# A gated mix of a recurrent attention and a feed-forward block: 32 output rows in one transfer instead of four

## The chip, the cores and the metric

The kernel runs on one core of a Trainium2 chip. Its measure is the time of one execution on the device, in microseconds (us). Five engines run side by side, each from its own instruction queue: TensorE (PE, with its weight loads as PEld), VectorE (DVE), ScalarE (ACT), GpSimd (POOL) and SyncE (SP). Data moves between device memory (HBM) and the on-chip memory of 128 partitions by DMA, on 16 DMA engines that all queues share. In this kernel SP issues the large weight loads, POOL nearly all small transfers.

## The reference

Two branches read the same 2048 rows of 1024 numbers and are mixed row by row with a gate.

```python
g = sigmoid((x * gate_w).sum(-1, keepdims=True))
return g * a + (1 - g) * b
```

Branch b is a feed-forward block, `gelu(x @ w_gate) * (x @ w_up) @ w_down`, with 3584 hidden units. Branch a is an attention that goes through the rows in 64 segments of 32, one after another, each with 8 rows of memory ahead of it:

```python
for s in range(n_seg):
    h = concatenate([mem, x[:, s*32:(s+1)*32, :]], axis=1)      # 8 + 32 rows
    q, k, v = h @ Wq, h @ Wk, h @ Wv                            # 32 heads of 128
    p = softmax(where(mask, q @ k.T * scale, -1e9))
    o = (p @ v) @ Wo
    mem = o[:, :8, :]
    outs.append(o[:, 8:, :])
```

The memory of a segment is the output of the one before, so the segments form a chain. All numbers are bfloat16 in HBM.

## The kernel before, in words

The first 600 us compute branch b for all rows and leave (1 - g) * b in a scratch tensor in HBM, `b_scr`, which is laid out by segment, column quarter and row. Then come the 64 segments, some 29 us each.

A segment keeps the 32 rows that are stationary for a matrix product in `hT`. The product has only 32 output rows, so four products run in four groups of 32 rows of a bank, one for each quarter of the columns. Hence the output of a segment stands in PSUM and in the tile `bo` as 128 partitions x 256 columns: partition 32 * q + r holds row r, columns 256 * q to 256 * q + 255.

The six projection weights and Wo do not fit on the chip. What stays lies in `arena`, `extra` and a few reused tiles; the rest streams through `ring`, ten slots of 1024 columns, in transfers of 512 or 256 KB that SP issues (`stream_next`, line 601) as soon as TensorE has freed a slot (`slot_free`, line 622). Each segment needs 18.5 units of 512 KB.

Of the 40 rows of a segment, 8 memory rows and 32 of its own, the block in `hT` holds rows 8 to 31 and then the memory rows; the output of the memory rows is the memory of the next segment. The first 8 rows of a segment do not hang on the recurrence as a projection does, and so their projections are made apart, for four segments at a time, by the jobs "q", "k" and "v" (the "ext" rows); the "o" job, in every fourth segment, makes the output of 32 ext rows, which goes through the tile `pn` (seen as `pnz`) that the softmax also writes (line 1045). The output of a segment leaves as the 32 rows `of[s * 32 + 8 : s * 32 + 40]`: the last 8 of them lie where the next segment's first rows belong, and the ext transfers (1343) write those rows afterwards, once the earlier transfers have landed.

The order of the work is written out by hand in the loop over s (line 798). Every operation is recorded by `op` with the keys that it reads and writes, and `_Sched` turns them into semaphore waits: an operation waits for the earlier writer of what it reads and for the earlier readers of what it writes. A DMA gets a semaphore of its own name (`dsem`), and whoever depends on it waits for the landing.

At the end of segment s the order is: ACT copies the accumulated output to `rows` (line 1306), TensorE transposes the memory rows (1317), DVE copies them into `hT` (1322), which lets TensorE go on with segment s + 1. Then DVE adds the gated output to `bo`, which holds (1 - g) * b (line 1325). POOL, which waits for that, issues the output transfers (1332), one for each column quarter: 32 partitions x 256 columns to 32 rows of `out`, 512 bytes each. With an "o" job DVE also writes `pn` (1336), and POOL issues four transfers of 32 ext rows (1343), whose side in HBM is 4 segments x 8 rows x 256 columns.

Behind these in POOL's queue stand, for segment s + 1: two loads of ext values into `vt` (723), one of ext queries and keys into `qkst` (711), a store of a job's result (852 or 877), and the load of the next `bo` (`load_b`, 737), which has to wait until the output transfers of segment s have read `bo`. Later in the segment come two more loads of `vt`, one of `qkst`, and that of the next rows into `hT` (412). The last segment issues its output from SP and ACT instead.

Of the kernel before, what the change touches and what calls it, by code (L numbers as in the profile page):

```python
# [26 lines left out]
class _Sched:  # L27
# [10 lines left out]
    def op(self, eng, mk, r=(), w=(), dsem=None):  # L38
        o = _Op(eng, mk, dsem)
        deps = []  # L40
        if eng == "pool" and dsem is None:
            w = [*w, ("pool",)]
        for k in r:
            deps += self.w.get(k, ())
            if k[0] == "P":
                deps += [x for x in self.r.get(k, ()) if x.eng != eng]
        for k in w:
            deps += self.w.get(k, ())
            deps += self.r.get(k, ())
        for k in r:  # L50
            self.r.setdefault(k, []).append(o)
        for k in w:
            self.w[k] = [o]
            self.r[k] = []
        seen = set()
        for d in deps:
            if d is o or id(d) in seen:
                continue
            seen.add(id(d))
            if d.eng == eng and d.dsem is None and (eng == "pe" or eng == "sp"):  # L60
                continue
            o.deps.append(d)
            d.sig = True
        self.ops.append(o)
        return o
# [63 lines left out]
def bass_gated_mix__memory_aug_recurrent_mem_tr__geglu_ffn__prompt_kernel(  # L129
# [16 lines left out]
    of = out.flatten_outer_dims()  # L146
# [4 lines left out]
    SEG = 32  # L151
# [12 lines left out]
    EXT = 8  # L164
# [3 lines left out]
    with ExitStack() as es:  # L168
# [14 lines left out]
        def SB(shape, dt, name):  # L183
            return es.enter_context(nc.sbuf_tensor(name, list(shape), dt))
# [17 lines left out]
        bo = SB([128, 256], BF16, "bo")  # L202
# [16 lines left out]
        def P(i):  # L219
            return ("P", i)  # L220

        g = _Sched()
        op = g.op
# [15 lines left out]
        def A(c):  # L239
# [6 lines left out]
           r=[("ident",)], w=[("ident",)])  # L246
# [57 lines left out]
        for b0 in (0, 64):  # L304
            op("pool", lambda e, b0=b0: e.affine_select(
                out=mask[b0:b0 + SEG, 0:NR], in_=mask[b0:b0 + SEG, 0:NR], compare_op=ALU.is_ge, fill=NEG,
# [3 lines left out]
                out=mask[b0 + SEG:b0 + L, SEG:L], in_=mask[b0 + SEG:b0 + L, SEG:L], compare_op=ALU.is_ge, fill=NEG,  # L310
# [3 lines left out]
        for side in range(2):  # L314
            op("pool", lambda e, side=side: e.memset(bm[64 * side:64 * side + L, side:side + 1], 1.0),
               r=[("bm",)], w=[("bm",)])
# [411 lines left out]
        def rows_of(s):  # L728
            n = SEG if s + 1 < NSEG else NR
            v = of[s * SEG + EXT:s * SEG + EXT + n, :]  # L730
            return [(v[:, q * 256:(q + 1) * 256], bo[32 * q:32 * q + n, :]) for q in range(4)]
# [12 lines left out]
        def first_rows(t, j, q):  # L744
            return t.rearrange("(g s r) d -> g s r d", s=GR, r=SEG)[j, :, 0:EXT, q * 256:(q + 1) * 256]
# [52 lines left out]
        for s in range(NSEG):  # L798
# [333 lines left out]
            if s == 0:  # L1132
                emit_P("q", 0, ALL[:5])
                op("pe", lambda e: e.matmul(PB[B_S][:, 0:320], lhsT=pnz[:, 0:128], rhs=pnz, start=True, stop=True),
                   r=[("init", "pn")], w=[P(B_S)])
# [10 lines left out]
                   w=[("bo", x) for x in range(4)])  # L1146
# [158 lines left out]
            if s + 1 < NSEG:  # L1305
                op("act", lambda e, B_O=B_O: e.activation(rows[:, 0:256], PB[B_O][:, 0:256], ACTF.Copy),
                   r=[P(B_O)], w=[("rows",)])
# [5 lines left out]
            if s + 1 < NSEG:  # L1313
# [12 lines left out]
                out=bo[:, :], in0=PB[B_O][:, 0:256], scalar=gseg[:, s:s + 1], in1=bo[:, :], op0=ALU.mult, op1=ALU.add),  # L1326
               r=[P(B_O)] + [("gseg", "%s%d" % (k, q)) for k in "ab" for q in range(4)], w=[("bo", x) for x in range(4)])
            for put, bank in ends:
                put(bank)
            last = s == NSEG - 1  # L1330
            for x, (d, b) in enumerate(rows_of(s)):
                op(("sp", "act")[x % 2] if last else "pool", lambda e, d=d, b=b: e.dma_start(d, b),  # L1332
                   r=[("bo", x)], w=[("out", s, x)], dsem="%s%d" % ("end" if last else "out", x))
            if "o" in jobs:
                j = jobs["o"]
                op("dve", lambda e, j=j: e.scalar_tensor_tensor(
                    out=pnz[:, 0:256], in0=PB[B_X][:, 0:256], scalar=ge[:, j:j + 1], in1=rowsx[:, 0:256],
                    op0=ALU.mult, op1=ALU.add),
                   r=[P(B_X)] + [("gseg", "e%d%d" % (q, u)) for q in range(4) for u in range(GR)] + RX,
                   w=[("pn", 0), ("pn", 2 * SEG)])  # L1340
                for q in range(4):
                    op(("sp", "act")[q % 2] if last else "pool",
                       lambda e, q=q, j=j: e.dma_start(first_rows(of, j, q), pnz[32 * q:32 * q + 32, 0:256]),
                       r=[("pn", 0)] + [("out", x, q) for x in range(max(0, j * GR - 1), j * GR + GR - 1)],
                       w=[("oute", j, q)], dsem="%s%d" % ("ende" if last else "oute", q))
# [43 lines left out]
```

## Time and profile before

| what | value |
|---|---|
| median of 3 runs | 2498.48 us (2494.85 to 2501.15) |
| profiled execution | 2490.87 us, of which the span is 2489.0 us |
| granted TensorE clock, mean | 0.988 |
| stretch 700 to 2440 us | PE busy 1539.88 us, POOL 533.10 us, DMA share 1.00, 367 GB/s |
| output transfers (line 1332) on POOL | 252 issues, 125.8 us |
| ext output transfers (line 1343) on POOL | 60 issues, 35.5 us |

A row of a group in the profile reads: line, engine, operation, tile written, tile read, count; then busy time and mean time of one; then the idle time of the engine just before these instructions and what ended it. A row of the list of waits reads: who waited for whom, us in total, times, longest. In the DMA row each digit is the mean busy share of the 16 DMA engines in one of 40 equal slices, 9 for 90% or more. The rows of queues give packets, MB, and the time of their packets as a share of 16 engines' span. A timeline row gives start and duration in us; one that ends in x4 stands for four instructions in a row. "To landing" is the time from the issue of a DMA to the last of the 16 increments of its semaphore.

### The profile page before, as it was taken

Reading aid. Unit: us, or ns where it says so; the run is one execution under the profiler, and the core shown is the slowest. Engines: PE = TensorE matmul, PEld = TensorE weight load, DVE = VectorE, ACT = ScalarE, POOL = GpSimd, SP = SyncE. Lnnn points to the kernel's source line nnn. Section 1 sums busy time; section 2 is a strip of 40 time slices with the busy share of each in tenths; the row PEclk is TensorE's granted clock in tenths of the full one; section 3 lists DMA queues with packets and bytes.
Section 4 is the critical chain, followed back from the end, with each engine's and each line's share of the span. In section 5 each row is a group of like instructions: output and inputs, shape, how many; then the busy total and the mean of one; then the engine's idle time right before and its main releaser. Section 6 shows DMA issues by size and latency. Waiting matters only on the chain.

```text
span 2489.0 us, 77539 instructions
## 1 busy us (share of the span) xinstructions
PE 2256.3 (91%) x33977; PEld 1112.8 (45%) x33977; DVE 1169.8 (47%) x3435; ACT 930.9 (37%) x2196; POOL 653.4 (26%) x1162
## 2 busy tenths in 40 slices
PE   9999999999889888988988898888889888889887
PEld 4444444444444444444444444444444444444443
DVE  5626264451444444544454544444444444455444
ACT  4314132221334343434443444434444434444433
POOL 1010103102232323233323323332323232323222
PEclk9999999999899999999999999999999999999988
DMA  8727354468999999999999999999999999999997
GB/s 273 257 71 256 97 179 123 144 229 302 322 348 365 365 371 348 373 359 379 375 377 354 374 366 374 352 356 367 375 370 378 365 363 376 362 377 374 371 362 281
DMA packets 328689, 797.10 MB, mean 320 GB/s; under 512 B 52728, under 2 KB 116456, under 8 KB 327584
## 3 DMA queue, kind: packets, MB, share of 16 engines
q1 hardware_dynamic: 284336, 736.78, 81.2%
q0 software_dynamic: 43872, 55.31, 7.1%
q8 instruction: 267, 4.37, 0.7%
q14 instruction: 70, 0.57, 0.1%
q10 hardware_dynamic: 144, 0.06, 0.0%
HBM read 764.52 MB, written 37.22 MB: 322 GB/s over the span
## 4 chain that ended last, share of the span: by engine, by line
PE 58%; DMA 26%; DVE 9%; ACT 4%; issue 3%; POOL 0%; SPq 0%; DVEq 0%; POOLq 0%
DMA ring<-w_scr 25%; PE pba L948 7%; PE pbb L948 7%; PE pbc L835 5%; PE pbb L1107 3%; PE pbe L1055 3%; PE pba L1107 2%; PE pbe L992 2%; PE pba L449 2%; PE pbb L449 2%; PE pbh L449 2%; PE pbg L449 2%; PE pbf L449 2%; PE pbe L449 2%; PE pbd L449 2%
## 5 line engine op out<-in xcount | busy, mean ns | idle before, releaser
L948 PE MATMUL pba<-arena,hT 128*32 128x512 bf16 x4416 | 350.6, 384 | 0.0
L948 PE MATMUL pbb<-arena,hT 128*32 128x512 bf16 x4416 | 342.6, 385 | 0.3 <-issue 0.3
L999 DVE COPY qk<-pbe 128x512 bf16<-128x512 bf16 x129 | 89.2, 692 | 363.3 <-PE pbe L992 358.6
L723 POOL DMA_DIRECT2D vt<-v_scr x252 | 147.9, 591 | 371.6 <-PE pbf L1066 234.1
L1038 ACT ACTIVATE pbd<-pbd 104x160 f32<-104x160 f32 x256 | 71.9, 281 | 432.2 <-DVE pbd L1036 432.2
L1060 DVE COPY ptb<-pbe 80x320 bf16<-80x320 bf16 x256 | 82.1, 321 | 240.5 <-PE pbe L1055 240.5
L1332 POOL DMA_DIRECT2D out_dram<-bo x252 | 125.8, 506 | 246.1 <-DVE bo L1325 244.9
L948 PE MATMUL pba<-ring,hT 128*32 128x512 bf16 x1542 | 153.2, 388 | 28.9 <-DMA ring<-w_scr 27.7
L835 PE MATMUL pbc<-arena,xe 128*32 128x512 bf16 x2208 | 174.4, 380 | 0.7 <-ACT rowsx L849 0.5
L948 PE MATMUL pbb<-ring,hT 128*32 128x512 bf16 x1536 | 151.9, 390 | 25.3 <-DMA ring<-w_scr 23.5
L954 ACT ACTIVATE rows<-pba 128x512 bf16<-128x512 f32 x128 | 76.6, 598 | 234.2 <-PE pba L948 234.2
L948 PEld LDWEIGHTS pba<-arena,hT 128*32 128x32 bf16 x4416 | 111.8, 97 | 97.9 <-issue 5.6
L1045 DVE TENSOR_TENSOR pn<-pbd,rr 104x256 bf16<-104x256 f32 (+1 forms) x512 | 142.3, 319 | 27.7 <-DMA out_dram<-pn 19.4
L948 PEld LDWEIGHTS pbb<-arena,hT 128*32 128x32 bf16 x4416 | 109.7, 97 | 93.0 <-issue 8.0
L954 ACT ACTIVATE rows<-pbb 128x512 bf16<-128x512 f32 x128 | 76.6, 598 | 173.7 <-PE pbb L948 173.6
L877 POOL DMA_DIRECT2D qk_scr<-rowsx x60 | 47.5, 791 | 344.2 <-DVE rowsx L874 281.6
L1107 PE MATMUL pba<-arena,oT 128*32 128x256 bf16 x2176 | 120.9, 281 | 14.1 <-ACT oT L1074 12.5
L1107 PE MATMUL pbb<-arena,oT 128*32 128x256 bf16 x2176 | 121.9, 279 | 12.7 <-ACT oT L1074 10.8
L1055 PE MATMUL pbe<-ident,pn 104*80 104x104 bf16 x1024 | 95.4, 216 | 40.9 <-DVE pn L1045 21.6
L1107 PE MATMUL pba<-ring,oT 128*32 128x256 bf16 x1792 | 107.0, 277 | 20.0 <-DMA ring<-w_scr 19.1
L1039 DVE TENSOR_REDUCE rs<-pbd 104x4 f32<-104x160 f32 x256 | 83.0, 324 | 88.9 <-ACT pbd L1038 88.9
L1107 PE MATMUL pbb<-ring,oT 128*32 128x256 bf16 x1792 | 113.5, 275 | 7.9 <-DMA ring<-w_scr 7.2
(260 smaller groups left out, 4355.2 us busy)
## 6 DMA issues: line engine op xcount, KB each, us to landing
ring<-w_scr SPq DMA_DIRECT2D x973, 512.0 KB, 6.3
ring<-w_scr SPq DMA_DIRECT2D x486, 256.0 KB, 5.9
arena<-in_B_w_gate_dram SPq DMA_DIRECT2D x27, 1024.0 KB, 5.5
arena<-in_B_w_up_dram SPq DMA_DIRECT2D x27, 1024.0 KB, 7.7
qkst<-qk_scr POOLq DMA_DIRECT2D x126, 64.0 KB, 5.2
qk_scr<-rowsx POOLq DMA_DIRECT2D x60, 128.0 KB, 5.6
arena<-in_B_w_down_dram SPq DMA_DIRECT2D x7, 1024.0 KB, 11.9
arena<-in_A_Wk_dram SPq DMA_DIRECT2D x6, 1024.0 KB, 6.9
```

The costliest lines, as they stand in the source:

```text
L449: ins = e.matmul(PB[bank][:, :], lhsT=wv[:, kc, col:col + 128], rhs=xb[:, kc, :], start=(kc == 0), stop=(kc == KC - 1))
L723: op("pool", lambda e: e.dma_start(vt[2 * SEG:KEYS, par, :], v_scr[s // GR, h, 2 * par:2 * par + 2, s % GR, :, :]), r=[("vscr", s // GR, h ...
L835: ins = e.matmul(PB[B_X][32 * gq:32 * gq + 32, :], lhsT=xe[:, us[-1], :], rhs=us[gq // 2][0][gq % 2], start=(n == 0), stop=(n == KC - 1), ...
L948: ins = e.matmul(PB[bank][32 * gq:32 * gq + 32, :], lhsT=hT[:, kc, :], rhs=us[gq // 2][0][gq % 2], start=(x == 0), stop=(x == KC - 1), ski ...
L954: op("act", lambda e: e.activation(rows[:, :], PB[bank][:, :], ACTF.Copy), r=[P(bank)], w=[("rows",)])
L999: op("dve", lambda e: e.tensor_copy(qk[:, m, :, 0:SEG, :], src), r=[P(B_T)], w=[("qk", m)])
L1039: op("dve", lambda e: e.tensor_reduce(rsv, sv, AX.X, ALU.add), r=[P(B_S)], w=[("rs",)])
L1045: op("dve", lambda e, c0=c0, k0=k0, n=n: e.tensor_tensor(out=pn[0:104, :, c0:c0 + 2 * n].rearrange("p i (two c) -> p i two c", two=2), in0 ...
L1055: ins = e.transpose(PBV[B_PT][0:KEYS, 512 + i * 128:512 + i * 128 + 104], pn[0:104, i, :], ident[0:104, 0:104])
L1060: op("dve", lambda e: e.tensor_copy(ptb[0:KEYS, :, :, :], src), r=[P(B_PT)], w=[("ptb",)] + first)
L1107: ins = e.matmul(PB[B_O][32 * q:32 * q + 32, 0:256], lhsT=oT[:, o % 2, k, :], rhs=u[q // 2][:, (q % 2) * 256:(q % 2 + 1) * 256], start=(o ...
L1332: op(("sp", "act")[x % 2] if last else "pool", lambda e, d=d, b=b: e.dma_start(d, b), r=[("bo", x)], w=[("out", s, x)], dsem="%s%d" % ("en ...
```

## The change

For all segments but the last, one transfer takes the place of four. Its source is the whole tile `bo`, 128 partitions x 256 columns; its destination is the same 32 rows of `out`, seen as 4 column quarters x 32 rows x 256 columns. It reads the four keys of `bo` and writes the four keys of `out`, so what depended on one of four semaphores now depends on `out0` alone. The last segment is as before.

```diff
-            for x, (d, b) in enumerate(rows_of(s)):
-                op(("sp", "act")[x % 2] if last else "pool", lambda e, d=d, b=b: e.dma_start(d, b),
-                   r=[("bo", x)], w=[("out", s, x)], dsem="%s%d" % ("end" if last else "out", x))
+            if last:
+                for x, (d, b) in enumerate(rows_of(s)):
+                    op(("sp", "act")[x % 2], lambda e, d=d, b=b: e.dma_start(d, b),
+                       r=[("bo", x)], w=[("out", s, x)], dsem="end%d" % x)
+            else:
+                op("pool", lambda e, s=s: e.dma_start(
+                    of[s * SEG + EXT:(s + 1) * SEG + EXT, :].rearrange("r (q c) -> q r c", q=4), bo[:, :]),
+                   r=[("bo", x) for x in range(4)], w=[("out", s, x) for x in range(4)], dsem="out0")
```

In the changed file the transfer stands in line 1336, and the ext output transfers move to line 1348. POOL's order is otherwise the same: `L1336 x1` where `L1332 x4` stood, and `L737` waits for one semaphore in place of four. No other engine's order changes.

## The prediction

> **What bounds the kernel now.** I read the page from the top: span, busy shares, DMA row and queues; then the groups that the diff touches and what they wait for; then one segment in order of time. The page first.
>
> ```profile
> span 2489.0 us, 77539 instructions
> PE 2256.3 (91%) x33977; PEld 1112.8 (45%) x33977; DVE 1169.8 (47%) x3435; ACT 930.9 (37%) x2196; POOL 653.4 (26%) x1162
> ...
> DMA  8727354468999999999999999999999999999997
> ...
> q1 hardware_dynamic: 284336, 736.78, 81.2%
> q0 software_dynamic: 43872, 55.31, 7.1%
> ...
> PE 58%; DMA 26%; DVE 9%; ACT 4%; issue 3%; POOL 0%; SPq 0%; DVEq 0%; POOLq 0%
> ...
> L1332 POOL DMA_DIRECT2D out_dram<-bo x252 | 125.8, 506 | 246.1 <-DVE bo L1325 244.9
> ```
>
> The list of DMA issues adds the size and the median time from issue to landing in us:
>
> ```profile
> out_dram<-bo POOLq DMA_DIRECT2D x252, 16.0 KB, 5.0
> out_dram<-pn POOLq DMA_DIRECT2D x60, 16.0 KB, 5.7
> ```
>
> From slice 10 on, where the segments run, the DMA row stands at 9. Asked for the stretch from 700 to 2440 us, the trace gives a DMA share of 1.00 at 367 GB/s and PE busy 1539.88 of 1740 us. So two resources are close to their limit: the 16 DMA engines, which mostly carry SP's weight stream (q1), and TensorE. The chain agrees: 58% PE, 26% DMA, and POOL 0%. The transfers that the change touches are issued by POOL (q0), which is idle for 246.1 us ahead of them, waiting for the last vector instruction of the segment. So their issue is off the path; what they can touch is the load of the DMA engines, and whoever waits for a POOL transfer. The list of waits, on that point:
>
> ```profile
> DVE pn L1045 <- DMA out_dram<-pn: 19.4, 13, 2.6
> ...
> POOL qkst L711 <- DMA out_dram<-bo: 5.3, 2, 2.7
> ...
> POOL bo L737 <- DMA out_dram<-bo: 0.6, 1, 0.6
> ```
>
> Nobody but POOL waits for the changed transfer, 5.9 us in all; VectorE waits 19.4 us over 13 segments for the extension rows (L1343) that stand behind it in POOL's queue. Now the boundary of one such segment in order of time:
>
> ```profile
> 1093.58 2.01 POOL L1332 DMA_DIRECT2D out_dram<-bo  x4 [10.90 <-DVE bo L1325]
> 1095.58 2.37 POOL L1343 DMA_DIRECT2D out_dram<-pn  x4
> 1097.94 1.14 POOL L723 DMA_DIRECT2D vt<-v_scr  x2
> ...
> 1098.30 0.10 PEld L948 LDWEIGHTS pba<-ring,hT 128*32 128x32 bf16 x4 [0.25 <-DMA ring<-w_scr]
> ...
> 1099.86 0.10 PEld L948 LDWEIGHTS pbb<-ring,hT 128*32 128x32 bf16 x4 [0.20 <-DMA ring<-w_scr]
> ...
> 1101.33 0.10 PEld L948 LDWEIGHTS pbb<-ring,hT 128*32 128x32 bf16 x4 [0.49 <-DMA ring<-w_scr]
> ...
> 1103.06 0.56 DVE L1045 TENSOR_TENSOR pn<-pbd,rr 104x256 bf16<-104x256 f32 x2 [1.25 <-DMA out_dram<-pn]
> ...
> 1104.71 0.24 PEld L1055 LDWEIGHTS pbe<-ident,pn 104*80 104x80 bf16 x4 [0.23 <-issue]
> ```
>
> The four issues take 2.01 us, and the first packets move 2.5 to 3 us after the first issue. Just then TensorE waits 0.2 to 0.5 us at a time for the weight ring. DVE's wait of 1.25 us for pn ends at 1103.06, pn is ready at 1103.62, and TensorE uses it only at 1104.71: that wait has 1.1 us to spare.
>
> **The change, part by part.** It removes 63 x 4 issues and puts in 63 x 1. The last segment's four, on SP and ACT, stay.
>
> *POOL's queue.* Four issues at 506 ns are 2.02 us a segment. The new one has 128 rows like the qkst load L711 (569 ns) and a four-part side like L1343 (599 ns); its lower bound is the 502 ns of 32 rows, its upper the 791 ns of L877, which has 128 x 4 pieces. I take 0.6 us, so what stands behind it issues 1.4 us earlier: the pn transfers in 15 segments, then vt and qkst. Behind vt and qkst nobody waits more than 0.6 and 0.5 us in total, so nothing comes of those. The pn wait of 19.4 us should fall to a few us (mean 1.5 us each, 1.4 us taken off). In the 15 segments the gap from pn ready to TensorE's use is 0.8 to 2.1 us in 14 and 0.05 us in one; in no more than that one does TensorE feel it. Taken: 0; ends: 0 and -19.4 us.
>
> *Load of the DMA engines.* In the packet records each L1332 leaves 16 packets of 1,024 bytes (2 rows, 46 ns each), one per engine, and 16 semaphore writes of 9 ns: per segment 64 x 46 + 64 x 9 = 3.5 engine-us. Each L1343, whose DRAM side has an outer dimension of 4, leaves 4 packets of 4,096 bytes instead, at 159 ns, and a 32-byte packet (13 ns) on each of 12 other engines. The new transfer's DRAM side is 4 x 32 x 256, so by that row it goes out as 4 engines x 4 packets: 16 x 159 to 178 ns (mean in this stretch) + 16 x 9 + 12 x 13 = 2.8 to 3.1 engine-us. Over 16 engines that is 25 to 40 ns a segment less, x 63 = -1.6 to -2.6 us where DMA is the bound. Taken: -2.
>
> *Their balance.* Before, each of 16 engines had 4 x 46 = 184 ns of it; now four engines would have 4 x 159 = 636 ns and twelve nearly nothing: 0.45 us late on four engines. A weight unit is complete when the last of its 16 increments lands, and those are spread over 2.15 us already (3.98 to 6.13 us after issue, medians of 1,459 transfers). Ends: 0, if the other engines' queued work (some 4 us between issue and first increment) lets the late four be made up for; 63 x 0.45 = +28 us, if each delay reaches TensorE and stays. The nearest row is vt's L723, whose source side is 2 x 8 x 512 and which puts 2 packets of 159 ns on each of two engines: ring transfers that meet it have spreads of 1.9 to 2.3 us, those that meet no POOL transfer 1.94. So a late pair moves the last landing by some 0 to 0.3 us for a lag of 0.32, and the engines stay busy at 1.00. I take a tenth of the upper end, +3 us.
> By the Trainium skill (DMA: Bandwidth & Descriptors, "Why a DMA increments its semaphore by 16 and not by 1", and "Rules for kernel authors") the number of engines is the largest that divides both sides' slowest dimension, here 4 of 128 and 4, and an outer dimension under 16 confines the whole DMA: the one rule that speaks against this change. The packet counts of L1343 and L723 agree with it. It adds that on the software path the engines come from a round-robin cursor; by that the late four rotate and the sum stays as above, while without it the fixed-set case below would stand. No view here names an engine.
>
> *Landing.* L1343 lands 5.7 us after issue with one packet per engine. Three more, each behind a weight packet of 159 to 178 ns, add about 1 us: 6.7 us, against 6.6 us from the first issue to the last landing of the four now. The load of bo (L737), which waited for four semaphores, now waits for one at about the same time; bo then lands 8.8 us or more ahead of its use. Behind L737 on POOL are vt and qkst, covered as above. Taken: 0.
> The same page ("Anatomy of one DMA") gives a fit of 2.0 us + bytes / 436e3 us for each transfer. By it four 16 KB transfers cost 8.1 us one after another and one of 64 KB 2.15 us, which would make the sum 63 x 5.95 = 375 us less if they stood on the path; the trace shows them overlapped and nobody waiting, so that sentence is worth nothing here.
>
> **Sum.** 0 - 2 + 3 + 0 = +1 us. The profiled execution took 2490.87 us (span 2489.0), 7.6 us under the median of the three runs, 2498.48; the change of +1 us is set on the median: 2499 us. About 0.3% (7.5 us) is what a measurement of this kernel can tell from no change.
>
> **Rivals.**
> (a) Slower: the four late engines. The place is 3 to 5 us after bo's write, where TensorE already waits for the ring; the price is up to 0.45 us a segment. It decides when more than 0.15 us of it (a third) stays, for 63 x 0.15 = 9.5 us. At half, 63 x 0.23 = +14 - 2, so 2511 us; the upper end is 2525. If the four engines are always the same ones, they carry 63 x 0.45 us more than the mean without recovery, and that upper end is the time. For it: DMA share 1.00, and PE waits for the ring in just that place. Against it: spread and queue depth as shown. Chance 0.32, of which 0.1 is the fixed set.
> (b) Faster: the shorter POOL queue counts after all, since the pn wait delays softmax and what follows it, and fewer small packets cost more than their busy time. Price up to 19.4 + 2.6 us; with two thirds of the pn wait, 13 + 2 us: 2483.5 us. For it: PE waits 21.6 us in total for pn (50 times, all segments). Against: the 1.1 us to spare. Chance 0.21.
> (c) The change does not gather on four engines: 16 packets of 4,096 bytes, one per engine. Then 159 in place of 184 ns and 27 ns of semaphore writes less on each: 63 x 0.05 = -3 us, so 2495 us. Against it: L1343's packets. Chance 0.08, inside "same".
>
> **How the numbers follow.** Forecast (within 0.3%) 0.39, (a) 0.32, (b) 0.21, (c) 0.08. Faster by over 0.3%: 0.21; within: 0.47; slower: 0.32. The forecast's own range is 2493 to 2505. The range for 8 in 10 takes in (b) as far as 2484 and (a) as far as 2521, which leaves out about a tenth at either end.
>
> **What would show it.** Right: L1336 with 63 issues of 0.55 to 0.65 us; landing 6 to 7.5 us; about 1,000 more 4,096-byte and 4,000 fewer 1,024-byte packets on q0; the pn wait of L1045 down from 19.4 to under 6 us; ring waits of L948 on both banks within a tenth of before. Wrong: ring waits (L948, L1107) longer by 10 us or more, a spread of the ring's increments over 2.4 us, or L737 waiting for out_dram. What would upset it most is a set of engines that doesn't rotate, which no view here shows.

## The result and the profile after

Over 20 runs each, the changed kernel takes 2505.78 us in the median, the kernel before 2495.93 us: a ratio of 1.0039, with a 95% interval of 1.0025 to 1.0053. That is 0.16 us for each of the 63 segments. The forecast was 2499 us. The time lies within the range for 8 in 10 (2484 to 2521) and just outside the forecast's own (2493 to 2505): the likeliest case did not come, rival (a) did, at a little over the point from which it decides, though the interval reaches under that point. The granted TensorE clock does not explain the difference: its mean is 0.991 over the changed kernel's 20 runs, and 0.989 to 0.990 over the runs of the kernel before that were taken beside the experiments. Runs of one kernel lie up to 25 us apart, so two single profiles can show what was done, and hardly the 10 us.

The page of the changed kernel, with the main rows that answer to those shown of before (line 1336 is the new transfer, and 1348 the ext output that was 1343):

```profile
span 2497.0 us, 77170 instructions
PE 2247.4 (90%) x33921; PEld 1112.8 (45%) x33977; DVE 1168.9 (47%) x3435; ACT 930.7 (37%) x2196; POOL 571.4 (23%) x973
...
q0 software_dynamic: 40848, 55.40, 7.1%
...
PE 57%; DMA 26%; DVE 9%; ACT 4%; issue 3%; POOL 0%; SPq 0%; DVEq 0%; POOLq 0%
```

The shares are those of before; POOL has 82 us less to do. The new transfer in the list of groups, and in the list of DMA issues with the time to landing:

```profile
L1336 POOL DMA_DIRECT2D out_dram<-bo x63 | 46.2, 733 | 239.9 <-DVE bo L1325 230.1 <-issue 9.8
```

```profile
out_dram<-bo POOLq DMA_DIRECT2D x63, 64.0 KB, 5.9
```

One issue takes 733 ns, so the queue is shorter by 4 x 506 - 733 = 1.3 us a segment. Queue q0 carries 3,024 packets fewer. The packet records divide them: 4,032 packets of 1,024 bytes and 63 x 48 = 3,024 semaphore writes are gone, 63 x 16 = 1,008 packets of 4,096 bytes and 3,024 of 32 bytes are new. Sixteen large packets a transfer and 48 small ones fit four engines with four large packets each, and 4 small ones on each of the other 12.

The list of waits of the changed kernel (total, times, longest):

```profile
PE pbb L948 <- DMA ring<-w_scr: 36.6, 52, 3.4
PE pba L948 <- DMA ring<-w_scr: 28.1, 47, 1.3
...
PE pba L1107 <- DMA ring<-w_scr: 15.1, 29, 1.5
...
PE pbb L1107 <- DMA ring<-w_scr: 5.1, 14, 0.8
...
DVE pn L1045 <- DMA out_dram<-pn: 2.8, 2, 1.8
...
POOL bo L737 <- DMA out_dram<-bo: 1.5, 1, 1.5
```

The same four rows of TensorE's waits for the ring, before:

```profile
PE pba L948 <- DMA ring<-w_scr: 27.7, 54, 1.3
PE pbb L948 <- DMA ring<-w_scr: 23.5, 51, 1.5
...
PE pba L1107 <- DMA ring<-w_scr: 19.1, 31, 1.4
...
PE pbb L1107 <- DMA ring<-w_scr: 7.2, 12, 1.8
```

The wait for pn has gone from 19.4 to 2.8 us, as it should with the shorter queue, and nothing came of it. TensorE's waits for the ring are 36.6 + 28.1 + 15.1 + 5.1 = 84.9 us; before they were 23.5 + 27.7 + 19.1 + 7.2 = 77.5. That is +7.4 us beside +8.0 us of span, in the right place but within what two profiles differ by. The same segment boundary as before, in order of time (start, duration; in brackets the wait ahead):

```profile
1094.14 0.69 POOL L1336 DMA_DIRECT2D out_dram<-bo  x1 [7.42 <-DVE bo L1325]
...
1094.82 2.33 POOL L1348 DMA_DIRECT2D out_dram<-pn  x4
...
1096.04 0.10 PEld L948 LDWEIGHTS pbb<-ring,hT 128*32 128x32 bf16 x4 [0.47 <-DMA ring<-w_scr]
...
1099.33 0.10 PEld L948 LDWEIGHTS pba<-ring,hT 128*32 128x32 bf16 x4 [0.56 <-DMA ring<-w_scr]
...
1100.85 0.10 PEld L948 LDWEIGHTS pbb<-ring,hT 128*32 128x32 bf16 x4 [0.18 <-DMA ring<-w_scr]
...
1102.63 0.10 PEld L948 LDWEIGHTS pbb<-ring,hT 128*32 128x32 bf16 x4 [0.79 <-DMA ring<-w_scr]
...
1102.87 0.56 DVE L1045 TENSOR_TENSOR pn<-pbd,rr 104x256 bf16<-104x256 f32 x2
...
1106.00 0.24 PEld L1055 LDWEIGHTS pbe<-ident,pn 104*80 104x80 bf16 x4 [0.23 <-issue]
```

L1325 starts here at 1093.37, 0.56 us later than in the profile of before. pn is ready without a wait, and TensorE asks for it 2.6 us afterwards. Four waits for the ring, of 0.47, 0.56, 0.18 and 0.79 us, stand in this stretch, where there were three, of 0.25, 0.20 and 0.49. So the gain (pn) is off the path, and the loss, if it is one, is in the ring. The experiments had to show that it is the number of engines that does it.

### The profile page after: what moved, and what is told of

Read it like the earlier page. It is cut to its first block, busy times and chain, and to the rows that moved or that the text cites. A ratio compares the mean times of both kernels' runs of the same rounds, so it can differ in the third digit from the quotient of the medians.

```text
span 2497.0 us, 77170 instructions
## 1 busy us (share of the span) xinstructions
PE 2247.4 (90%) x33921; PEld 1112.8 (45%) x33977; DVE 1168.9 (47%) x3435; ACT 930.7 (37%) x2196; POOL 571.4 (23%) x973
## 4 chain that ended last, share of the span: by engine, by line
PE 57%; DMA 26%; DVE 9%; ACT 4%; issue 3%; POOL 0%; SPq 0%; DVEq 0%; POOLq 0%
DMA ring<-w_scr 25%; PE pba L948 8%; PE pbb L948 7%; PE pbc L835 5%; PE pbb L1107 3%; PE pbe L1055 2%; PE pbe L992 2%; PE pba L1107 2%; PE pba L449 2%; PE pbb L449 2%; PE pbd L449 2%; PE pbg L449 2%; PE pbc L449 2%; PE pbh L449 2%; PE pbf L449 2%
## 5 line engine op out<-in xcount | busy, mean ns | idle before, releaser
L948 PE MATMUL pba<-arena,hT 128*32 128x512 bf16 x4416 | 349.3, 383 | 0.3 <-issue 0.3
L948 PE MATMUL pbb<-arena,hT 128*32 128x512 bf16 x4416 | 341.2, 384 | 0.3 <-issue 0.3
L948 PE MATMUL pbb<-ring,hT 128*32 128x512 bf16 x1536 | 151.4, 387 | 39.2 <-DMA ring<-w_scr 36.6
L948 PE MATMUL pba<-ring,hT 128*32 128x512 bf16 x1542 | 153.3, 386 | 29.9 <-DMA ring<-w_scr 28.1
L948 PEld LDWEIGHTS pba<-arena,hT 128*32 128x32 bf16 x4416 | 111.7, 97 | 96.4 <-issue 3.7
L948 PEld LDWEIGHTS pbb<-arena,hT 128*32 128x32 bf16 x4416 | 109.6, 97 | 90.8 <-issue 4.7
L1045 DVE TENSOR_TENSOR pn<-pbd,rr 104x256 bf16<-104x256 f32 (+1 forms) x512 | 142.0, 319 | 11.6 <-DMA out_dram<-pn 2.8
L711 POOL DMA_DIRECT2D qkst<-qk_scr x126 | 70.5, 560 | 224.6 <-DVE qk L1011 223.3
L1107 PE MATMUL pba<-ring,oT 128*32 128x256 bf16 x1792 | 106.2, 276 | 15.7 <-DMA ring<-w_scr 15.1
L1055 PEld LDWEIGHTS pbe<-ident,pn 104*80 104x80 bf16 x1024 | 62.3, 116 | 129.1 <-DVE pn L1045 65.6
```

The lines of the kernel that those rows point to most:

```text
L948: ins = e.matmul(PB[bank][32 * gq:32 * gq + 32, :], lhsT=hT[:, kc, :], rhs=us[gq // 2][0][gq % 2], start=(x == 0), stop=(x == KC - 1), ski ...
L1045: op("dve", lambda e, c0=c0, k0=k0, n=n: e.tensor_tensor(out=pn[0:104, :, c0:c0 + 2 * n].rearrange("p i (two c) -> p i two c", two=2), in0 ...
L1055: ins = e.transpose(PBV[B_PT][0:KEYS, 512 + i * 128:512 + i * 128 + 104], pn[0:104, i, :], ident[0:104, 0:104])
L1107: ins = e.matmul(PB[B_O][32 * q:32 * q + 32, 0:256], lhsT=oT[:, o % 2, k, :], rhs=u[q // 2][:, (q % 2) * 256:(q % 2 + 1) * 256], start=(o ...
```

## The experiments

Three theories were on the table: (I) the gathering on four engines delays the ring; (II) the shorter POOL queue sends what stands behind it into a crowded moment; (III) one transfer of 64 KB costs more than four of 16 KB however it is spread.

**The same transfer, in three views of its destination.** It goes to a scratch tensor, where the same 64 KB can be cut in several ways:

```diff
-    of[s * SEG + EXT:(s + 1) * SEG + EXT, :].rearrange("r (q c) -> q r c", q=4), bo[:, :]),
+    o_scr[s, :].rearrange("(p c) -> p c", c=256), bo[:, :]),               # scr_k16: 128 x 256
+    o_scr[s, :].rearrange("(r q c) -> q r c", q=4, c=256), bo[:, :]),      # scr_k4: 4 x 32 x 256
+    o_scr[s, :].rearrange("(r q c) -> q r c", q=2, c=256), bo[:, :]),      # scr_k2: 2 x 64 x 256
```

Expected of scr_k16:

> The segment's output goes as one POOL transfer from 128 partitions to a contiguous 64 KB scratch, whose side is 128 rows x 256, so 16 packets of 4,096 bytes, one per engine; the rows of out that it should write are left out. One issue as in the changed kernel, POOL's queue as short as there. Theory I (the price is the gathering on four engines): back to the kernel before or a little under, ratio to before 0.997 to 1.001. Rival II (the price is the shorter POOL queue, which sends the transfers behind it earlier into a crowded moment): as slow as the changed kernel, 1.003 to 1.005. Rival III (one transfer of 64 KB costs more than four of 16 KB, however it is spread): 1.003 to 1.005.

Expected of scr_k4:

> As scr_k16, into the same 64 KB of scratch, but the destination is seen as 4 x 32 x 256: 4 engines with 4 packets of 4,096 bytes. It is the control for the scratch. Theory I: as the changed kernel, 1.0025 to 1.0055. Rivals II and III: the same as scr_k16, whatever that gives. If the place in HBM matters (rows of out against scratch), it differs from the changed kernel and equals scr_k16.

Expected of scr_k2:

> As scr_k16, into the same 64 KB of scratch, seen as 2 x 64 x 256: 2 engines with 8 packets of 4,096 bytes, 8 x 159 = 1.27 us on each. The changed kernel paid (2505.78 - 2495.93) / 63 = 0.16 us a segment for a lag of 0.45 us, a third. Theory I: a third or more of 1.2 us stays, 63 x 0.4 = 25 us or more, ratio 1.008 to 1.02, and the spread of the ring's landings grows again. Rivals II and III: the same as scr_k4 and scr_k16 within 0.2%.

| kernel | large packets per engine | ratio to before, 95% interval | packets of 32 bytes more than scr_k16 | issue, mean | landing |
|---|---|---|---|---|---|
| scr_k16 | 1 on each of 16 | 1.0004 (0.9982 to 1.0026) | 0 | 552 ns | 5.0 us |
| scr_k4 | 4 on each of 4 | 1.0031 (1.0010 to 1.0052) | 3,024 = 63 x 12 x 4 | 733 ns | 5.7 us |
| scr_k2 | 8 on each of 2 | 1.0102 (1.0072 to 1.0132) | 7,056 = 63 x 14 x 8 | 841 ns | 7.0 us |

All three have the same bytes in the same place and one issue each. The time goes up with the gathering, and the 128-row view costs no more than four transfers. Theories II and III are out as the cause: they had all three alike, and they had scr_k16 at 1.003 to 1.005. The clear step is that to scr_k2; the intervals of scr_k16 and scr_k4 overlap, but the means of their 12 runs each lie 8.0 us apart, with some 5 us either way. The scratch gives what the rows of `out` gave (1.0031 against 1.0039). The four ring rows of the list of waits, of scr_k16 and then of scr_k2 (lines 949 and 1108 are here what 948 and 1107 were):

```profile
PE pbb L949 <- DMA ring<-w_scr: 39.3, 60, 1.7
PE pba L949 <- DMA ring<-w_scr: 31.1, 50, 1.6
PE pba L1108 <- DMA ring<-w_scr: 14.4, 27, 1.6
PE pbb L1108 <- DMA ring<-w_scr: 4.9, 11, 0.8
```

```profile
PE pbb L949 <- DMA ring<-w_scr: 47.1, 73, 2.7
PE pba L949 <- DMA ring<-w_scr: 38.0, 65, 1.5
PE pba L1108 <- DMA ring<-w_scr: 12.6, 25, 1.2
PE pbb L1108 <- DMA ring<-w_scr: 7.3, 13, 1.2
```

They sum to 89.7 and 105.0 us, +15.3 us where the profiled executions differ by 13.9 (2507.01 and 2520.88 us; the medians, 2495.50 and 2524.96, differ by more, because the profiled scr_k16 was one of its slower runs). TensorE's waits for other things did not grow beside it. For the step to scr_k4 the profiles are too coarse: its four rows sum to 91.3 us, 1.6 more than in scr_k16, in an execution that was 3.6 us shorter (2503.46 us).

**No output at all.** The branch that issues the transfer is taken out.

> The output transfers of all segments but the last are left out, so those rows of out are not written. It prices the whole of them. By the load alone (3.5 engine-us a segment over 16 engines, 63 x 0.22 = 14 us) where the DMA engines are the bound: 2482 us, ratio 0.994. If the engines have slack: 0.998 to 1.0. Theory I puts it close to scr_k16, within 0.6%; rival II (a shorter POOL queue harms) as slow as or slower than the changed kernel less 14 us, so 0.998.

Measured: 0.9990 (0.9970 to 1.0009). The whole output costs 2.5 us, and not more than 7.5 us, where its busy time on 16 engines would make 14 us. So a DMA share of 1.00 did not mean here that each nanosecond of engine time counts (without the output the share still reads 0.99), and there was never much to gain from lighter packets.

**Is the weight ring the way?** In light_k16 and light_k2, from the second segment on, only half of each ring transfer is loaded, so the ring is in time; the rest is scr_k16 and scr_k2.

```diff
-    ring[...].rearrange("p a b -> p (a b)"), src[:, a * 1024:b * 1024]),
+    ring[...].rearrange("p a b -> p (a b)")[:, 0:(b - a) * 1024 // half], src[:, a * 1024:a * 1024 + (b - a) * 1024 // half]),   # half = 2 if s else 1
```

> scr_k16 with half of each transfer of the weight stream left out from the second segment on (the other half of the slots keeps stale weights, so the results are not the reference's). The ring then comes in time. TensorE is busy for 1540 of 1740 us and waits some 2 us a segment for other things than the ring, 1.3 us for the ring: about 63 x 1.3 = 80 us less, ratio 0.960 to 0.975 under every theory. It is the partner of light_k2.

> light_k16 with the output seen as 2 x 64 x 256, on two engines, as in scr_k2. If the price of the gathering goes by way of the weight ring (a late engine delays the last landing of a unit that TensorE is waiting for), it is gone or nearly so: within 0.15% of light_k16. If it goes another way (the landing of the output, the load of bo behind it, writes that block other work), the 24 us between scr_k2 and scr_k16 stay: 0.8% or more above light_k16.

Measured: 0.9502 (0.9489 to 0.9515) and 0.9528 (0.9514 to 0.9542), medians 2372.87 and 2379.30 us. light_k16 came out faster than the 0.960 to 0.975 expected: beside the ring waits of 89.7 us, TensorE's busy time went down by 51 us (2253.3 us in scr_k16, 2202.4 in light_k16). Some 15 us of that is the granted clock, 0.987 against 0.993; the rest suggests that "busy" had held some of the waiting. With a quieter ring, gathering on two engines costs 6.4 us in place of some 24 (0.0098 x 2497). Three quarters are gone; it was to be under 0.15% and is 0.26%. What is left is the same wait: light_k16 has no row of TensorE's matmuls waiting for the ring, and light_k2 has these three, 10.8 us in all, beside 11.3 us between the two profiled executions:

```profile
PE pba L950 <- DMA ring<-w_scr: 4.7, 6, 1.4
PE pbb L950 <- DMA ring<-w_scr: 3.9, 6, 1.2
PE pba L1109 <- DMA ring<-w_scr: 2.2, 1, 2.2
```

So the price shrinks with the ring's load, and what is left of it stands in the ring's waits. The DMA share fell too, from 1.00 to 0.65 between 700 and 2440 us, so whatever else queues at the DMA engines had an easier time as well; that the price is paid in the waits for the ring rests on these rows and those of scr_k2.

**Always the same engines, or a set that moves on?** Four transfers of 64 KB a segment, to four scratch areas, each as 128 x 256 or as 4 x 32 x 256:

```diff
+    for z in range(4):
+        op("pool", ... o_scr[z, s, :].rearrange("(p c) -> p c", c=256) ...               # x4_k16
+        op("pool", ... o_scr[z, s, :].rearrange("(r q c) -> q r c", q=4, c=256) ...      # x4_k4
```

> The output tile goes four times a segment, each time as one POOL transfer of 64 KB to its own contiguous scratch, 128 rows x 256: each of 16 engines gets 4 packets of 4,096 bytes. The rows of out are left out. It is the partner of x4_k4, with the same bytes, issues and addresses. The load alone: 4 x 159 = 0.64 us per engine and segment, against 0.16 us in scr_k16; if all of the rise counts, 63 x 0.48 = 30 us, ratio 1.012; as the whole output costs nearly nothing by noout, about 1.002 to 1.012.

> As x4_k16, but each of the four is seen as 4 x 32 x 256 and so goes to four engines. If the set of engines moves on by four from one transfer to the next, the four of a segment together load all 16 engines alike and the ratio is that of x4_k16 within 0.3%. If it is always the same set, four engines get 16 packets of 159 ns = 2.5 us in a burst, twice scr_k2's lag on twice the engines: ratio at least 0.015 above x4_k16.

Measured: 1.0067 (1.0045 to 1.0090) and 1.0161 (1.0141 to 1.0181). The difference, 0.94%, lies between the two marks of the expectation and decides nothing. The ring rows of x4_k4,

```profile
PE pba L949 <- DMA ring<-w_scr: 57.5, 94, 2.2
PE pbb L949 <- DMA ring<-w_scr: 44.6, 74, 2.4
PE pba L1108 <- DMA ring<-w_scr: 11.2, 24, 1.2
PE pbb L1108 <- DMA ring<-w_scr: 10.4, 20, 1.3
```

sum to 123.7 us, against 40.4 + 35.9 + 13.2 + 7.0 = 96.5 in x4_k16: +27.2 us, where the two profiled executions differ by 30.1 us (2537.36 and 2507.31) and the medians by 26.2 (2537.36 and 2511.18). Again the ring holds most of the difference. To see the engines themselves, large transfers were put behind the kernel's last output, where nothing else runs:

```diff
+    for grp, (eng, q) in enumerate((("pool", 4), ("pool", 2), ("sp", 4))):
+        for z in range(4):
+            op(eng, ... t_scr[y, :].rearrange("(r q c) -> q r c", q=q, c=2048), chunk(0)[:, 0:2048] ...
```

> The changed kernel, and behind its last output twelve transfers of 512 KB (128 partitions x 4 KB) to scratch, on engines that have nothing else to do: four from POOL seen as 4 x 32 x 4 KB, then, when these have landed, four from POOL seen as 2 x 64 x 4 KB, then four from SP seen as 4 x 32 x 4 KB. On four engines one of them takes 32 x 159 ns = 5.1 us, on two 10.2 us. If the set of engines moves on from transfer to transfer, the four of a group run side by side: each lands about 2 + 5 = 7 us (12 us for two engines) after its own issue. If the set is always the same, they queue: 7, 12, 17, 22 us from the first issue (12, 22, 33, 43 us for two engines). x4_k4, which cost 0.9% over x4_k16, leaves both open: 0.3% was expected of the first and 1.5% of the second.

Measured in one execution, from the semaphore records (16 increments for a transfer of POOL; for one of SP five records, one at its issue and four later):

```
group              increments that came with no data ahead of them   last increment, us from the group's first issue
POOL, 4 engines    12, 8, 4, 0                                       11.6, 13.6, 16.7, 16.9
POOL, 2 engines    14, 12, 10, 8                                     15.6, 18.0, 18.4, 18.9
SP, 4 engines      (one record at the issue)                         10.4, 15.3, 20.3, 25.3
```

On POOL every engine posts an increment for every transfer, behind whatever it still has queued. The first transfer of the first group leaves 12 engines free, which post by 2.2 us; the second finds 8 free, the third 4, the fourth none. (The counts are read from the times: the eighth of the second came at 4.2 us, the fourth of the third at 7.1, each ahead of the rest.) So each takes four other engines, and the group of two moves on by two. On SP the transfers land 5 us after one another, which is 32 x 159 ns, as they would on always the same four. The landing times of POOL's groups alone would not have told it, since the first takes 11.6 us and not 7. The fixed set is out for this kernel. The Trainium skill (DMA: Bandwidth & Descriptors, "Why a DMA increments its semaphore by 16 and not by 1") states both: a round-robin cursor on the software path, and the lowest-numbered engines on the hardware path. These runs agree with the first and with there being one fixed set on SP; which engines it is, they don't show.

**Does the place in the segment matter?** The segment's transfer is left out, and one from the same tile is issued in the middle of the next segment, behind the load of hT:

```diff
+    load_x(s + 1)
+    if s > 0:
+        op("pool", ... o_scr[s, :] in the view of scr_k16 or scr_k2, bo[:, :] ...
```

> The segment's output transfer is left out; in its place the tile bo, then holding only its loaded part, goes to scratch in the middle of the next segment, behind the load of hT, some 20 us after the segment's start in place of 0.8 us, as one transfer of 128 rows x 256 on 16 engines. It is the partner of late_k2, 0.997 to 1.002.

> As late_k16, seen as 2 x 64 x 256: two engines with 8 packets each, as in scr_k2, served some 22 to 26 us into the segment. There TensorE waits for the ring 0.01 to 0.06 us in each microsecond in the kernel before, against 0.14 to 0.16 at 3 to 5 us, and 1 us of other waits follows at the segment's end. If the price hangs on the place (rival (a) of the prediction put it where TensorE waits for the ring), late_k2 lies less than 0.5% above late_k16. If each delay stays wherever it falls, it lies about 1.0% above it, as scr_k2 above scr_k16.

Measured: 1.0008 (0.9981 to 1.0036) and 1.0083 (1.0052 to 1.0115). The difference is 0.75%, against 0.98% for the pair at the start of the segment; with about 0.4% of uncertainty on each, they can't be told apart, and the mark of 0.5% is neither met nor ruled out. The list of waits does not follow here: the four ring rows sum to 32.8 + 26.9 + 20.4 + 6.6 = 86.7 us in late_k16 and 37.3 + 27.0 + 18.3 + 9.7 = 92.3 us in late_k2, +5.6 us where the profiled executions differ by 22.5 us (2497.67 and 2520.20). TensorE's busy time is longer by 11.6 us (2252.6 and 2264.2), but the granted clocks differ as well, 0.990 and 0.986. Where late_k2 pays its price is not shown.

**The same cure on another transfer.** If two late engines cost something, the four vt loads of a segment should gain from being spread. The kernel before, with another layout of the scratch:

```diff
-    v_scr = nc.dram_tensor("v_scr", [NG, 2, 4, GR, EXT, 512], BF16)
+    v_scr = nc.dram_tensor("v_scr", [NG, 2, GR, 4, EXT, 512], BF16)
-    v_scr[s // GR, h, 2 * par:2 * par + 2, s % GR, :, :]),
+    v_scr[s // GR, h, s % GR, 2 * par:2 * par + 2, :, :].rearrange("g r c -> (g r) c")),
...
-    op("pool", ... v_scr[j, h, :, :, :, :].rearrange("g u r c -> (g u r) c"), rx ...
+    for g in range(4):
+        op("pool", ... v_scr[j, h, :, g, :, :], rx[32 * g:32 * g + 32, :] ...
```

> The kernel before, with its four output transfers, but the layout of the scratch for ext values changed so that each of the four vt loads of a segment reads 16 rows of one stretch: 16 x 1 KB on 16 engines in place of 2 x 8 x 1 KB on two engines with 2 packets of 4,096 bytes each. The store of that scratch becomes four transfers of 32 partitions, each 4 x 8 x 1 KB. If gathering on few engines is what costs, the four pairs with a lag of 0.3 us each cost about as much as one transfer with a lag of 0.5 us on four engines (0.1 us) or more: 63 x 0.1 to 0.3 = 6 to 19 us faster, ratio 0.992 to 0.998. If such small lags are made up, 0.999 to 1.001; the 31 x 3 more stores weigh nothing on POOL.

Measured: 1.0011 (0.9987 to 1.0035), medians 2497.28 and 2497.12 us. No gain: a miss for the simple form of theory I, in which every lag has its price. But the edit did more than the expectation weighed. The store of the scratch, 32 transfers of 128 rows before, became 128 whose HBM side begins with 4, and these gather in their turn: the trace has 8 packets of 4,096 bytes and 24 of 16 bytes for each, as with two large packets on each of four engines and two small ones on each of the other twelve. (The 16-byte packets of q0 fall from 7,184 to 3,200, which is 252 x 28 fewer and 128 x 24 more.) So gathered stores took the place of gathered loads, and what the loads' lags of 0.3 us cost by themselves is not shown.

No version that does all of the work was found to beat the kernel before. The 128-row view, which costs no more, can't be had for the real output: its HBM side needs an outer dimension of 4, because `bo` holds the column quarters one below the other.

## Why the prediction was right or wrong

*What bounds the kernel.* TensorE and the weight stream, with POOL off the path: right; with half of the stream left out the time falls by 5%. The reading of the DMA share was too strict. Without any output the kernel gains 2.5 us and not 14.

*POOL's queue.* 1.3 us shorter for 1.4 forecast; 733 ns an issue, inside the ends of 502 and 791 but not the 600 taken. The table of the three views shows what it goes with: the time of an issue grows with the gathering, from 552 to 733 to 841 ns. The pn wait fell to 2.8 us (under 6 forecast) and was worth nothing, as taken. Rival (b) is out with it; scr_k16, which has the short queue and no gathering, is at 1.0004.

*Load of the engines.* -2 us was taken; scr_k16, with the lighter packets, shows +1 us with about 5.5 either way, so no gain is shown. The count was right in the large packets and wrong in the small: 4 packets of 32 bytes on each idle engine, not one.

*Balance.* This is the step that failed, in its size. The mechanism, four engines with 4 packets each (rival (a), without its fixed set), is what the packets show, and (c) is out. The prediction put the lag at 0.45 us and took a tenth of it, +3 us, since a moving set and queued work should make the rest up. Measured: 0.16 us a segment by the change itself, 0.27% or 6.7 us between scr_k4 and scr_k16, so a quarter to a third of the lag stays. With scr_k2 it is 0.39 us of 1.1, a third. The set does move, so that part of the reasoning stood, and the loss is there all the same. So the range held because rival (a) was in it, and not because the forecast's sum was right.

*The signs.* The packets came as named. The ring waits of L948 were to stay within a tenth of before on both banks: 27.7 became 28.1 us, but 23.5 became 36.6. The four ring rows grew by 7.4 us, under the 10 that were to show the forecast wrong. The spread of the ring's increments, which the prediction put at 2.15 us, is 2.21 us with the change (the same medians over all ring transfers), under its mark of 2.4. It grows in every pair: 2.12 in scr_k16, 2.31 in scr_k4 and 2.29 in scr_k2; 2.20 and 2.30 in the x4 pair; 2.19 and 2.36 in the late pair; 1.10 and 1.22 in the light pair. That agrees with theory I, where a late engine delays the last landing of a unit; noout, with no output at all, stands at 2.21, so 0.1 us is also what executions differ by.

*Landing.* 5.9 us for 6.7 forecast; L737 waited once, 1.5 us. Covered, as taken.

What stays open is why a lag that moves from engine to engine is not made up. x4_k4 loads all 16 engines alike within about 3 us and still costs 26 us more than x4_k16; late_k2 pays 0.75% (0.33 to 1.17) where the ring is less waited for. That a unit of weights needs all 16 engines at every moment, so that each lag counts while it lasts, fits these runs; it is argued, not shown, and vt16, which could have spoken against it, put gathered stores in the place of gathered loads. The packets of 32 bytes always come with the gathering and were not separated from it; by their busy time (15 ns each) they make 0.06 us on an idle engine in scr_k4 and 0.12 us in scr_k2. In x4_k4 each engine gets 12 of them a segment, 0.18 us, and 63 x 0.18 = 11 us would be a good part of the 26, if all of it counted.

## What to carry to other kernels

Fewer and larger transfers are no gain by themselves when nobody waits for their issue or landing: here the four issues and the wait behind them were free. Before merging transfers, look at the outermost dimension on both sides: here an HBM side that began with 128, 4 or 2 went to 16, 4 or 2 engines, and 128 partitions on the other side did not help. The price of gathering on few engines did not stand in the waits for the transfer itself but mostly in those for the big stream beside it: look for it there, and in the whole time over many runs.

## What the runs showed that was not expected

- Engines that have no data of a POOL transfer still get small packets: 4 of 32 bytes each with four engines, 8 with two.
- POOL needs longer to issue the same 64 KB the fewer engines it goes to: 552, 733 and 841 ns.
- A DMA share of 1.00 over 1740 us left room for a transfer of 64 KB a segment at a cost within 2.5 us, where its packets' time came to 14 us; three more of them (x4_k16 against scr_k16) cost 0.63%, 15.7 us, of 30 by their packets' time. The share adds up the packets' times, and these overlap: in the trace of before more than 16 packets are open at once for a third of the stretch from 700 to 2340 us.
- Transfers of one group from POOL run on sets of engines that move on, and from SP, it seems, on the same set: four of 512 KB landed within 17 us on POOL and 5 us apart on SP.
